# The first four row blocks of v, made by half-height matmuls in two PSUM banks

## The chip, the cores and the metric

The kernel runs on one core of a Trainium2 chip. The metric is the device time of one execution in microseconds (us). The engines are TensorE (PE for its matmuls and PEld for its weight loads, in the profile), VectorE (DVE), ScalarE (ACT), GpSimd (POOL) and SyncE (SP), which issues most of the DMAs. PSUM, into which TensorE writes, has eight banks of 128 partitions x 512 float32.

## The reference

A gate mixes two branches over the same x (2048 rows of 512 columns): a Fourier mixing layer, and sliding-window attention with 32 heads of 16 columns and a window of 256 rows.

```python
def reference(A_x, A_dft_seq_re, A_dft_seq_im, A_dft_hid_re, A_dft_hid_im, B_x, B_wqkv, B_wo, gate_w):
    x = A_x
    g = _sigmoid((x * gate_w).sum(-1, keepdims=True))
    a = _A_ref(x, A_dft_seq_re, A_dft_seq_im, A_dft_hid_re, A_dft_hid_im)   # Real(DFT_seq(DFT_hidden(x)))
    b = _B_ref(x, B_wqkv, B_wo)
    return g * a + (1 - g) * b

def _B_ref(x, wqkv, wo):          # H = 32, Dh = 16, W = 256
    q, k, v = split(x @ wqkv)
    scores = q @ k.T * Dh ** -0.5
    mask = (i - j >= 0) & (i - j < W)
    p = _softmax(where(mask, scores, -1e9))
    return concat_heads(p @ v) @ wo
```

The change touches one product of it alone: v, which is x times the last 512 columns of wqkv, and of its 2048 rows the first 512.

## The kernel before

Every large product is made in float32r, a float32 form that TensorE takes in one pass. To keep precision each operand is split into a rounded part `hi` and a rest `lo`, and three products are summed in PSUM: hi*hi, hi*lo and lo*hi (`TERMS`, L253). x stands in SBUF transposed, in four pieces of 128 contraction rows (`dk`) for each quarter `ss` of the 2048 rows: `XT[dk, ss]` holds hi and lo of such a piece. A block `sb` of v is 128 rows of x (column slice `c` of quarter `ss`) by 512 columns, so it takes 4 pieces x 3 terms = 12 matmuls of 128 contraction rows, a weight block of 128 columns and 512 moving columns, all into one PSUM bank (`row_proj`, L303, the matmul on L309; its tile is called `dv` for v, and `dab` for the Fourier products, which use the same lines). ACT then copies the bank to an SBUF tile `ev` (L320) and SP stores that to the scratch `v_scr` in DRAM (L321).

PSUM is shared out by pools: `ps_a` has four banks (tag `st`, tiles `s` and `t` of the attention), `ps_o` two, `ps_d` two (tag `d`, tiles `dv`, `dqk`, `dab`, `dc`, used in turn).

The program's dense work is one generator, `dense` (L601). It starts with ten matmuls on zeros (`warm`), then the first q and k projection (`qk_first`, 24 matmuls into two banks of `ps_a`), and then, for each quarter of x, the q and k projection (`qk_proj`, from the second quarter on) and four blocks of v. PE, ACT, DVE and SP run in the order in which the code emits the work (`manual_schedule`). The first attention step comes after `need(("v", 5))` (L1003), so up to there PE has dense matmuls only: q and k of the first quarter, v blocks 0 to 3, q and k of the second quarter, v blocks 4 and 5. Later, every few dense matmuls are followed by one of the attention's score matmuls (L372, tile `s`), transposed score matmuls (L454, tile `t`) or a set of its products with v (L480, tile `o`).

While v blocks 0 to 3 run, small jobs are taken from a list (`job`, called after each matmul with its number): one split of a piece of the next quarter's x per block (`x_job`), in which ACT makes `hi` (L80) and DVE makes `lo` (L85). These pieces, `XT[0..3, 1]`, are what the q and k projection right behind the four blocks reads.

The sets of L480 are the only matmuls of the program that use part of TensorE's array: for the four heads `p` of a group, a weight block of 128 rows x 32 columns each, written to the PSUM partitions 32p to 32p+31.

Of the kernel before, what the change touches and what calls it, by code (L numbers as in the profile page):

```python
# [7 lines left out]
F32 = mybir.dt.float32  # L8
# [6 lines left out]
P = 128  # L15
S = 2048
D = 512
DK = D // P
# [14 lines left out]
def fnet_window_mix(ctx: ExitStack, tc: tile.TileContext, xT, x, wqk, wv, wr, wi, cr, ci, wo, gw, out):  # L33
    nc = tc.nc
# [3 lines left out]
    st = ctx.enter_context(tc.tile_pool(name="st", bufs=3))  # L38
    ev = ctx.enter_context(tc.tile_pool(name="ev", bufs=5))
    at = ctx.enter_context(tc.tile_pool(name="at", bufs=2))  # L40
    ps_a = ctx.enter_context(tc.tile_pool(name="ps_a", bufs=4, space=PSUM))
    ps_o = ctx.enter_context(tc.tile_pool(name="ps_o", bufs=2, space=PSUM))
    ps_d = ctx.enter_context(tc.tile_pool(name="ps_d", bufs=2, space=PSUM))
# [4 lines left out]
    v_scr = [dram.tile([2, P, 2, NG, 64], F32, name=f"v_scr{i}") for i in range(8)]  # L48
# [6 lines left out]
    def ld(dst, src):  # L55
        mark("sp", nc.sync.dma_start(dst, src))

    def f(ap):
        return ap.bitcast(F32)
# [4 lines left out]
    def mark(e, ins):  # L64
        last[e] = ins.ins
# [30 lines left out]
    def load_raw(src):  # L96
        raw = st.tile([P, 1024], F32, name="raw", bufs=2)
        ld(raw, src)
        return raw
# [11 lines left out]
    def split_soon(raw, on_dve=False):  # L111
        hi = st.tile([P, 1024], F32R, name="hi")
        lo = st.tile([P, 1024], F32R, name="lo")
        for c in HALVES:
            jobs.append(lambda c=c: late(nc.scalar.copy if FIN else (nc.vector if masks else nc.gpsimd).tensor_copy,
                                         hi[:, c], raw[:, c]))
            jobs.append(lambda c=c: late((nc.vector if on_dve or masks else nc.gpsimd).tensor_sub, lo[:, c], raw[:, c], f(hi[:, c])))
        return hi, lo

    def job(n):  # L120
        if n == 2 and ended:
            ended.pop(0)()
        if n % 6 == 3 and jobs:
            jobs.pop(0)()
# [4 lines left out]
    XT = {}  # L129
# [17 lines left out]
    with tc.manual_schedule(engines={mybir.EngineType.Activation, mybir.EngineType.DVE, mybir.EngineType.SP}):  # L147
# [11 lines left out]
        for dk in range(DK):  # L159
            c = slice(dk * 256, dk * 256 + 256)  # L160
# [92 lines left out]
    TERMS = ((0, 0), (0, 1), (1, 0))  # L253
# [25 lines left out]
    def qk_proj(g, ss, w):  # L279
        for i in range(2):  # L280
            ps = ps_d.tile([P, 512], F32, name="dqk", tag="d")
            n = 0
            for dk in range(DK):
                c = dk * 256 + i * 128
                for a, b in TERMS:
                    nc.tensor.matmul(ps, w[a][:, c:c + 128], XT[dk, ss][:, b],  # L286
                                     start=n == 0, stop=n == 11)
                    n += 1
                    job(n)
                    if n < 12:  # L290
                        yield
            qk_evict(g, ss, i, ps)
            yield
# [9 lines left out]
    def row_proj(sb, w, ps):  # L303
        n = 0
        ss, c = divmod(sb, 4)
        for dk in range(DK):
            wh = [w[dk // 2][h][:, (dk % 2) * 512:(dk % 2) * 512 + 512] for h in range(2)]
            for a, b in TERMS:
                nc.tensor.matmul(ps, XT[dk, ss][:, a, c * 128:(c + 1) * 128], wh[b],  # L309
                                 start=n == 0, stop=n == 11)  # L310
                n += 1
                job(n)
                if n < 12:
                    yield

    def v_proj(sb, w):
        ps = ps_d.tile([P, 512], F32, name="dv", tag="d")
        yield from row_proj(sb, w, ps)
        t = ev.tile([P, 512], F32, name="ev")
        mark("act", nc.scalar.copy(t, ps))  # L320
        ld(v_scr[sb // 2][sb % 2].rearrange("r a g x -> r (a g x)"), t)  # L321
        yield

    def load_ab(i, sc):
        t = big.tile([P, 2, 512], F32R, name="big")
        ld(f(t[:]), ab_scr[i][sc])
        return t
# [263 lines left out]
    def late(fn, *args):  # L591
        with behind("act", "dve"):
            return fn(*args)  # L593
# [7 lines left out]
    def dense():  # L601
# [5 lines left out]
        wvs = [late(split_raw, r, True) for r in wraw]  # L607
# [4 lines left out]
        def x_job(ss, dk):  # L612
            late(split_x, ss, (dk,), ss == 1 or (None if ss == 3 else False))
            if dk % 2 and ss == 2:
                load_x(3, dk // 2)

        for ss in range(4):
            if ss < 3:
                for dk in range(DK):
                    jobs.append(lambda ss=ss, dk=dk: x_job(ss + 1, dk))  # L620
                    jobs.append(lambda: None)
            if ss:
                yield from qk_proj(0, ss, wq0)
            if ss == 3:
                w = split_soon(raw, True)
                jobs[:] = [j for split in jobs for j in (split, lambda: None)]
            for c in range(4):
                yield from v_proj(ss * 4 + c, wvs)
                have.add(("v", ss * 4 + c))
                if c == 1:  # L630
                    have.add(("qk", 0, ss))
                if ss == 2 and c == 2:
                    raw = load_raw(wqk[1])
                    wraw = [load_raw(wi[0])]
# [3 lines left out]
        for g in range(1, NG):  # L638
# [37 lines left out]
            if g < 3:  # L676
                w = nextw
# [20 lines left out]
        for sc in range(4):  # L698
            ab[sc] = load_ab(0, sc)
# [24 lines left out]
        def next_b():  # L724
            if next(calls) * 8 % (2 * SWITCH) >= 8:
                return
            sc = todo_b.pop(0)
            with behind("sp"):
                nxt[sc] = load_ab(1, sc)
# [235 lines left out]


    stream = dense()
    quota = 0.0

# [150 lines left out]
```

## Time and profile before

| | |
|---|---|
| time, median of 3 runs | 844.1 us (843.34 to 844.24) |
| the profiled execution: its own time / its span | 843.79 us / 841.8 us |
| v blocks 0 to 3 on PE | 11.0 to 21.9 us from the span's start |
| PE busy, matmuls and weight loads | 837.9 us in 5322 and 698.4 us in 5322 instructions |
| DVE, ACT, POOL busy | 643.1, 610.1, 294.9 us |

A row of a timeline gives the start, the time from the first start to the last end, the engine, the line of the kernel, the operation with the tile it writes and those it reads, and how many instructions were merged. What stands in square brackets is the idle time of the engine before it, and what ended that. A matmul's own duration contains its way through the array, so matmuls in a row overlap; how fast they follow each other is read from their starts. The chain of waits gives the same work without that overlap.

### The profile page before, as it was taken

Reading aid. Unit: us, or ns where it says so; the run is one execution under the profiler, and the core shown is the slowest. Engines: PE = TensorE matmul, PEld = TensorE weight load, DVE = VectorE, ACT = ScalarE, POOL = GpSimd, SP = SyncE. Lnnn points to the kernel's source line nnn. Section 1 sums busy time; section 2 is a strip of 40 time slices with the busy share of each in tenths; the row PEclk is TensorE's granted clock in tenths of the full one; section 3 lists DMA queues with packets and bytes.
Section 4 is the critical chain, followed back from the end, with each engine's and each line's share of the span. In section 5 each row is a group of like instructions: output and inputs, shape, how many; then the busy total and the mean of one; then the engine's idle time right before and its main releaser. Section 6 shows DMA issues by size and latency. Waiting matters only on the chain.

```text
span 841.8 us, 17198 instructions
## 1 busy us (share of the span) xinstructions
PE 837.9 (100%) x5322; PEld 698.4 (83%) x5322; DVE 643.1 (76%) x2084; ACT 610.1 (72%) x1832; POOL 294.9 (35%) x604
## 2 busy tenths in 40 slices
PE   9999999999999999999999999999999999999998
PEld 8888888888888888888888887878888878878997
DVE  5588977777879787787877876878987867656974
ACT  6488888878888897787877877867877865553330
POOL 8101333233332233342323243343143357756410
PEclk9999999999999999999999999999999999999999
DMA  8776678485756183533454557969864256456632
GB/s 301 249 225 205 209 237 282 158 273 194 231 206 197 46 235 111 175 116 122 140 163 124 167 160 221 299 217 317 277 200 155 96 175 196 143 195 203 206 133 93
DMA packets 94491, 161.03 MB, mean 191 GB/s; under 512 B 26816, under 2 KB 35520, under 8 KB 94400
## 3 DMA queue, kind: packets, MB, share of 16 engines
q1 hardware_dynamic: 93968, 159.28, 58.9%
q8 instruction: 42, 0.69, 0.3%
q10 hardware_dynamic: 432, 0.66, 0.2%
q14 instruction: 49, 0.40, 0.1%
HBM read 108.27 MB, written 51.64 MB: 190 GB/s over the span
## 4 chain that ended last, share of the span: by engine, by line
PE 100%; DVE 0%; issue 0%
PE dc L534 42%; PE dab L309 11%; PE dqk L286 10%; PE t L454 9%; PE s L372 9%; PE o L480 8%; PE dv L309 5%; PE t L929 5%; PE s L274 1%; PE dv L599 1%; PE s L392 0%; PE t L564 0%; DVE rt L566 0%
## 5 line engine op out<-in xcount | busy, mean ns | idle before, releaser
L534 PE MATMUL dc<-big,hi 128*128 128x512 f32 x1020 | 344.3, 393 | 0.0
L374 DVE CUSTOM_DVE_ANT_0 sm<-s,mask 128x320 f32<-128x320 f32 (+4 forms) x512 | 235.1, 464 | 111.0 <-PE s L372 71.1
L377 ACT ACTIVATE sm<-sm,ml 128x320 f32<-128x320 f32 (+4 forms) x512 | 277.3, 543 | 56.2 <-DVE ml L374 52.4
L455 ACT ACTIVATE pt<-t 128x320 f32<-128x320 f32 (+4 forms) x392 | 159.5, 411 | 83.5 <-PE t L454 78.2
L534 PE MATMUL dc<-big,lo 128*128 128x512 f32 x510 | 200.0, 392 | 0.0
L534 PEld LDWEIGHTS dc<-big,hi 128*128 128x128 f32 x1020 | 179.4, 188 | 21.2
L459 POOL TENSOR_SCALAR_AFFINE_SELECT pt<-pt 128x128 f32<-128x128 f32 x196 | 75.7, 386 | 278.2 <-ACT pt L455 276.1
L454 PE MATMUL t<-ring,pad 128*128 128x320 f32 (+4 forms) x512 | 156.6, 306 | 0.0
L372 PE MATMUL s<-ring,pad 128*128 128x320 f32 (+4 forms) x512 | 155.0, 303 | 0.0
L355 DVE TENSOR_SCALAR pad<-ring,half 96x256 fp32r<-96x256 f32 x384 | 118.7, 356 | 5.2 <-PE t L454 4.9
L454 PEld LDWEIGHTS t<-ring,pad 128*128 128x128 f32 x512 | 96.0, 188 | 30.4 <-issue 8.7
L372 PEld LDWEIGHTS s<-ring,pad 128*128 128x128 f32 x512 | 96.2, 188 | 20.3 <-DVE ml L374 0.7
L534 PEld LDWEIGHTS dc<-big,lo 128*128 128x128 f32 x510 | 95.9, 188 | 11.9
L593 DVE TENSOR_TENSOR lo<-raw,hi 128x512 fp32r<-128x512 f32 x139 | 95.9, 697 | 2.5 <-ACT hi L593 2.4
L377 ACT ACTIVATION_READ_ACCUMULATOR sm<-sm,ml 128x1 f32 x512 | 97.3, 190 | 0.0
L309 PE MATMUL dab<-hi,big 128*128 128x512 f32 x256 | 88.9, 394 | 0.0
L286 PE MATMUL dqk<-big,hi 128*128 128x512 f32 x240 | 85.0, 393 | 0.0
L437 POOL TENSOR_SCALAR vpad<-vr,half 128x256 f32<-128x256 f32 x64 | 62.1, 981 | 60.4 <-PE o L480 29.5
L353 ACT ACTIVATE pad<-ring,half 96x256 fp32r<-96x256 f32 x128 | 66.8, 522 | 0.0
L459 POOL TENSOR_SCALAR_AFFINE_SELECT home<-home 128x128 f32<-128x128 f32 x60 | 33.9, 565 | 89.8 <-ACT home L455 85.3
L463 POOL TENSOR_SCALAR_AFFINE_SELECT pt<-pt 128x128 f32<-128x128 f32 x172 | 63.0, 366 | 0.0
L593 DVE CAST hi<-raw 128x512 fp32r<-128x512 f32 x126 | 53.9, 435 | 11.9 <-PE dc L534 10.6
(121 smaller groups left out, 1034.0 us busy)
## 6 DMA issues: line engine op xcount, KB each, us to landing
qk_scr<-home SPq DMA_DIRECT2D x32, 512.0 KB
ring<-qk_scr SPq DMA_DIRECT2D x32, 512.0 KB
raw<-cr SPq DMA_DIRECT2D x32, 512.0 KB
raw<-ci SPq DMA_DIRECT2D x32, 512.0 KB
r_scr<-ev SPq DMA_DIRECT2D x42, 256.0 KB
ab_scr<-home SPq DMA_DIRECT2D x20, 512.0 KB
big<-ab_scr SPq DMA_DIRECT2D x20, 512.0 KB
ring<-qk_scr SPq DMA_DIRECT2D x32, 256.0 KB
```

The source lines that it names most:

```text
L286: nc.tensor.matmul(ps, w[a][:, c:c + 128], XT[dk, ss][:, b], start=n == 0, stop=n == 11)
L309: nc.tensor.matmul(ps, XT[dk, ss][:, a, c * 128:(c + 1) * 128], wh[b], start=n == 0, stop=n == 11)
L355: mark(f"pad{i}", nc.vector.tensor_scalar(dst, src, half[:96, h:h + 1], None, op0=OP.mult))
L372: nc.tensor.matmul(ps[:, :w], PAD[0, n][:, p], ring[1][:, p, k0:k0 + w], start=True, stop=True)
L374: mark("dve", nc.vector.tensor_tensor_reduce(out=sm[:, :w], in0=ps[:, :w], in1=mask[:, WIN - w:], scale=1.0, scalar=3e38, op0=OP.add, op1= ...
L377: mark("act", nc.scalar.activation(sm[:, :w], sm[:, :w], AF.Exp, bias=nm[:, c], scale=-1.0, accum_out=l[:, c]))
L454: nc.tensor.matmul(ps[:, :w], PAD[1, n][:, p], ring[0][:, p, q0:q0 + w], start=True, stop=True)
L455: nc.scalar.activation(pt[:, p, :w], ps[:, :w], AF.Exp, scale=-1.0)
L459: nc.gpsimd.affine_select(a, a, pattern=[[0, 2], [2, 64]], compare_op=OP.is_ge, fill=0.0, base=1, channel_multiplier=-1)
L480: nc.tensor.matmul(OT[g, sb][32 * p:32 * p + 32, q - sb * 512:e - sb * 512], v2[:, p], pt[:, p, q - q0:e - q0], start=first, stop=kb == 8 ...
L534: nc.tensor.matmul(ps, w[a][:, i % 8 * 128:i % 8 * 128 + 128], ab[SC[i]][:, b], start=i == ends[0] and a + b == 0, stop=i == ends[1] and a ...
L593: return fn(*args)
```

## The change

Blocks 0 to 3 of v go through a new function. It takes a second PSUM bank, from `ps_a`, and cuts each of the twelve matmuls in two: contraction rows 0 to 63 into the first bank, rows 64 to 127 into the second. `tile_position` puts the two on the upper and on the lower half of TensorE's array. At the end ACT copies the first bank, as before, and DVE adds the second bank to it. All other blocks of v keep the old function.

```diff
+    def v_first(sb, w):
+        ps = ps_d.tile([P, 512], F32, name="dv", tag="d"), ps_a.tile([P, 512], F32, name="s", tag="st")
+        n = 0
+        ss, c = divmod(sb, 4)
+        for dk in range(DK):
+            for a, b in TERMS:
+                for i in range(2):
+                    r = slice(64 * i, 64 * i + 64)
+                    nc.tensor.matmul(ps[i], XT[dk, ss][r, a, c * 128:(c + 1) * 128],
+                                     w[dk // 2][b][r, (dk % 2) * 512:(dk % 2) * 512 + 512],
+                                     start=n == 0, stop=n == 11, tile_position=(64 * i, 0))
+                n += 1
+                job(n)
+                if n < 12:
+                    yield
+        t = ev.tile([P, 512], F32, name="ev")
+        mark("act", nc.scalar.copy(t, ps[0]))
+        mark("dve", nc.vector.tensor_add(t, t, ps[1]))
+        ld(v_scr[sb // 2][sb % 2].rearrange("r a g x -> r (a g x)"), t)
+        yield
+
...
             for c in range(4):
-                yield from v_proj(ss * 4 + c, wvs)
+                yield from (v_proj if ss else v_first)(ss * 4 + c, wvs)
                 have.add(("v", ss * 4 + c))
```

On PE, the end of the last of the four blocks and the first row of the projection behind it; `dv` is the bank from `ps_d`, `s` the one from `ps_a`, `hi` and `lo` are the weights of v, and `big` the piece of x. Before:

```order
L309 MATMUL dv_440<-hi_332,big_249 128x512
L309 MATMUL dv_440<-hi_332,big_256 128x512
L309 MATMUL dv_440<-lo_333,big_256 128x512
L309 MATMUL dv_440<-hi_332,big_256 128x512
L286 MATMUL dqk_459<-big_378,hi_230 128x512 x2
```

and with the change:

```order
L332 MATMUL dv_482<-hi_332,big_249 128x512
L332 MATMUL s_483<-hi_332,big_249 128x512
L332 MATMUL dv_482<-hi_332,big_256 128x512
L332 MATMUL s_483<-hi_332,big_256 128x512
L332 MATMUL dv_482<-lo_333,big_256 128x512
L332 MATMUL s_483<-lo_333,big_256 128x512
L332 MATMUL dv_482<-hi_332,big_256 128x512
L332 MATMUL s_483<-hi_332,big_256 128x512
L286 MATMUL dqk_515<-big_382,hi_230 128x512 x2
```

Each matmul has become two, which write different banks in turn; over the four blocks that is 96 where there were 48. The rows of PE before and behind the four blocks are the same in both programs.

On DVE, between the first quarter's q and k and the second's, the L85 rows that read `pt` make the `lo` of x's second quarter (tiles `big`), and the L82 and L85 rows that read `raw` split its third quarter. With the change:

```order
L90 TENSOR_TENSOR home_304<-s_339,home_304 128x512 [waits Activation_49]
L85 TENSOR_TENSOR big_382<-pt_322,big_382 128x512 [waits DMAHW1_49,Activation_49]
L341 TENSOR_TENSOR ev_403<-ev_403,s_375 128x512 [waits PE_49,Activation_49]
L85 TENSOR_TENSOR big_415<-pt_322,big_415 128x512 [waits Activation_49]
L341 TENSOR_TENSOR ev_436<-ev_436,s_408 128x512 [waits PE_49,Activation_49]
L85 TENSOR_TENSOR big_457<-pt_324,big_457 128x512 [waits DMAHW2_49,Activation_49]
L341 TENSOR_TENSOR ev_478<-ev_478,s_441 128x512 [waits PE_49,Activation_49]
L85 TENSOR_TENSOR big_490<-pt_324,big_490 128x512 [waits Activation_49]
L341 TENSOR_TENSOR ev_511<-ev_511,s_483 128x512 [waits PE_49,Activation_49]
L82 CAST big_519<-raw_370 128x512 [waits DMAHW3_49]
```

The four L341 rows are new; without them the list is that of before. Each waits for PE and for ACT's copy, and has the next split of x behind it.

On SP, the stores of v, and the loads into `ring` (q and k of the first quarter, from which the attention starts); the rows with a minus are those of before:

```order
 L56 DMA qk_scr_0_0_97<-home 128x2x512 [waits DMAHW6_49,DVE_49]
-L56 DMA v_scr_113<-ev 128x512 [waits Activation_49] x2
+L56 DMA v_scr_113<-ev 128x512 [waits DVE_49] x2
 L56 DMA ring_264<-qk_scr_0_0_81 64x4x512 [waits DMAHW5_49,DMAHW1_49]
-L56 DMA ring_264<-qk_scr_0_0_81 32x4x512 [waits DMAHW2_49]
-L56 DMA ring_265<-qk_scr_0_0_97 32x4x512 [waits DMAHW6_49,DMAHW3_49]
+L56 DMA ring_265<-qk_scr_0_0_97 32x4x512 [waits DMAHW6_49,DMAHW2_49]
+L56 DMA ring_264<-qk_scr_0_0_81 32x4x512 [waits DMAHW3_49]
```

The stores of v wait for DVE where they waited for ACT, and two of the ring's four loads have changed places.

## The prediction

> **What bounds the kernel now.** I read the page's busy times and its chain of waits first, since they say which engine the end hangs on, then the chain in the first 60 us, where the change sits, and then the timelines of PE, DVE and ACT there.
>
> ```profile
> PE 837.9 (100%) x5322; PEld 698.4 (83%) x5322; DVE 643.1 (76%) x2084; ACT 610.1 (72%) x1832; POOL 294.9 (35%) x604
> PEclk9999999999999999999999999999999999999999
> PE 100%; DVE 0%; issue 0%
> 11.18 10.88 PE dv L309 x48
> 22.06 5.44 PE dqk L286 x24
> ```
>
> The first row counts busy time by engine, the second is the clock that TensorE was granted in 40 slices (full speed in all), the third the chain that ended last: all of it is PE. So the time is the sum of what PE's instructions take, one behind the other, and a microsecond more or less on PE anywhere is a microsecond at the end. The last two rows are the chain where the change is: the 48 matmuls of v's blocks 0 to 3 take 10.88 us, which is 226.7 ns each, and the 24 of the next projection 5.44 us, the same 226.7 ns. PE waits for nothing there. Other engines matter only if they come too late for it.
>
> **What a matmul consists of.** PE's timeline in two places gives the parts. The first three rows are from where the attention starts, with a score matmul of 64 columns among those of v; the last two from a later stretch, with 320 columns.
>
> ```profile
> 33.01 0.19 PE L372 MATMUL s<-ring,pad 128*128 128x64 f32 x1
> 33.04 0.47 PE L309 MATMUL dv<-lo,big 128*128 128x512 f32 x1
> 33.35 0.62 PE L309 MATMUL dv<-hi,big 128*128 128x512 f32 x2
> ...
> 120.32 0.31 PE L454 MATMUL t<-ring,pad 128*128 128x320 f32 x1
> 120.47 0.62 PE L309 MATMUL dab<-hi,big 128*128 128x512 f32 x2
> ```
>
> 320 columns hold PE for 0.15 us and 512 for 0.227, so a column costs (0.227 - 0.15) / 192 = 0.40 ns, 512 columns 0.205 us, and about 0.02 us of a matmul is fixed. The 64-column matmul and the one behind it take 33.35 - 33.01 = 0.34 us together, where columns and fixed parts would ask for 0.03 + 0.23 = 0.26: the weights of the second were not there yet. A load of 128 weight columns therefore needs about 0.03 + 0.08 = 0.11 us, and behind a matmul of 512 columns (0.227 us) it is hidden.
>
> **The change on PE.** 48 matmuls go, 96 come. Each has half the contraction rows, but the same 128 weight columns and the same 512 moving columns; nothing above says that rows cost time, and columns do. Alone, each should cost what L309 costs now. The question on which everything hangs is whether the two of a pair run side by side, on the two halves of the array. The trace has one group that does run side by side, the products with v on quarters of the array. Here is one such group with its neighbours, eight sets of four:
>
> ```profile
> 116.85 0.39 PE L309 MATMUL dab<-hi,big 128*128 128x512 f32 x1
> 117.17 2.36 PE L480 MATMUL o<-pt,vpad 128*32 128x320 f32 x32
> 119.46 0.41 PE L454 MATMUL t<-ring,pad 128*128 128x320 f32 x1
> 119.71 0.31 PE L372 MATMUL s<-ring,pad 128*128 128x320 f32 x1
> 119.86 0.39 PE L309 MATMUL dab<-hi,big 128*128 128x512 f32 x1
> ```
>
> 32 matmuls in 2.36 us from first start to last end is 0.27 to 0.29 us for a set of four, although one alone, with its own duration of 0.43 us, would not be through: four overlap. So PE can run tiles side by side. But that group differs from the pair in two ways. Its four write to 32 PSUM partitions each, all different, so that together each partition gets one stream of 320 values in some 0.27 us. The pair of the change writes two banks of the same 128 partitions, so side by side each partition must take 2 x 512 values in 0.227 us, more than three times the rate of that row and twice that of L309; no row of the trace shows this. And the group is plain float32, with 0.27 us for 320 columns against 0.15 us for the float32r of the rest; every float32r matmul in the trace uses the whole array. So the price of a pair is bounded from both sides: as much as one matmul now (side by side), or twice that (one behind the other). By operands, type, columns and the partitions written, the row nearest to a half is L309 itself, and I take twice:
>
> - the pairs: 48 x (2 x 226.7 - 226.7) ns = 48 x 0.2267 = +10.9 us;
> - two changes of the array's layout. From whole to quarters, 117.17 - 116.85 = 0.32 us where 0.227 is usual, 0.09 lost, and with 128 weight columns (that group has 32) up to 0.11 us of load that nothing hides. Back, the last set starts 2.36 - 0.43 = 1.93 us after 117.17, so at 119.10; L454 follows after 0.36 us in place of 0.27, 0.09 lost, and the next matmul comes 0.25 us later where 320 columns take 0.15, 0.10 lost: 0.2 + 0.2 = +0.4 us.
>
> The sum is made against the profiled execution's own 843.79 us (its span is 841.8, and 2.0 lie around it): 843.79 + 10.88 + 0.4 = 855.1 us. The median shown is 844.1, 0.3 above that execution. If the fixed part falls away in a tile, a pair takes 2 x 0.205, +8.8 in place of +10.9: 853.0. If each half adds some 0.01 us, +1.0: 856. So 853 to 856 in this case.
>
> The Trainium skill says otherwise. Its page "TensorE: Matmul & The Clock Gate", section "Part 3: Packing small matmuls — row/col tiling", has matmuls on different row groups of the array run concurrently, and gives 3.07 times the speed for four tiles of 32 rows at 512 columns. By it a pair would cost about what one matmul costs now, and the sum would be 844.2 us; that is the first rival. The trace agrees for tiles that share the columns out (L480, four in 0.27 us), and no run here shows it for tiles that share the rows out, nor for float32r.
>
> **The change on the other engines.** DVE gets four adds of 128 x 512 out of PSUM; the nearest row is L90, 0.68 us each. Their dates are tightest if PE keeps its pace, so I check them there; with slower pairs every block of PE comes 2.7 us later than the one before it and there is more room. DVE, then ACT:
>
> ```profile
> 12.18 0.68 DVE L92 SCALAR_TENSOR_TENSOR home<-s,home 128x512 fp32r<-128x512 f32 x1
> 12.78 0.68 DVE L90 TENSOR_TENSOR home<-s,home 128x512 fp32r<-128x512 f32 x1
> 13.38 0.68 DVE L85 TENSOR_TENSOR big<-pt,big 128x512 fp32r<-128x512 f32 x1
> 15.08 0.69 DVE L85 TENSOR_TENSOR big<-pt,big 128x512 fp32r<-128x512 f32 x1 [1.02 <-ACT big L80]
> 20.19 0.70 DVE L85 TENSOR_TENSOR big<-pt,big 128x512 fp32r<-128x512 f32 x1 [4.42 <-ACT big L80]
> 21.19 0.69 DVE L85 TENSOR_TENSOR big<-pt,big 128x512 fp32r<-128x512 f32 x1 [0.31 <-ACT big L80]
> 21.80 0.42 DVE L82 CAST big<-raw 128x512 fp32r<-128x512 f32 x1
> 25.45 0.69 DVE L92 SCALAR_TENSOR_TENSOR home<-dqk,home 128x512 fp32r<-128x512 f32 x1 [2.50 <-ACT home L88]
> ```
>
> ```profile
> 16.66 0.59 ACT L320 COPY ev<-dv 128x512 f32<-128x512 f32 x1 [1.61 <-PE dv L309]
> 20.06 0.58 ACT L320 COPY ev<-dv 128x512 f32<-128x512 f32 x1
> 22.10 0.59 ACT L320 COPY ev<-dv 128x512 f32<-128x512 f32 x1 [0.94 <-PE dv L309]
> ```
>
> The adds fall into the idle 1.02, 4.42 and 2.50 us. The third one, after ACT's copy at 20.64 and DVE's L85 at 20.89, ends at 21.57 and moves the last L85 from 21.19 to 21.57, so the last `lo` of x's second quarter is there at 22.3. PE reads that in the tenth to twelfth matmul of the projection that starts at 22.06, so not before 22.06 + 10 x 0.227 = 24.3: 2 us to spare. If that cover were gone, the price would be 0.4 us, once. The fourth add (copy done at 22.69, so 23.4) has L82 and L85 behind it, which are through by 24.5, before L92 at 25.45. The new PSUM banks are those of the first projection; DVE has read them out by 13.5, and the third block, first to take one again, starts after 16.
>
> SP's stores of v wait 0.7 us longer, and the loads of `ring` stand behind two of them.
>
> ```profile
> L56 SPq DMA_DIRECT2D ring<-qk_scr x4: 566/617/787, 19.3 to 21.2; - x4
> 30.91 0.60 DVE L355 TENSOR_SCALAR pad<-ring,half 96x256 fp32r<-96x256 f32 x2
> 33.24 0.23 DVE L374 CUSTOM_DVE_ANT_0 sm<-s,mask 128x64 f32<-128x64 f32 x1 [1.73 <-PE s L372]
> ```
>
> The loads are issued at 19.3 to 21.2; the second store's data would be there at 17.25 + 0.68 = 17.9, still before. Whoever reads the ring (L355, at 30.91) did not wait for it, and after that DVE waits 1.73 us for PE. So these edits cost nothing.
>
> **The rivals.** *Side by side* (not slower): the second of a pair starts while the first streams, on its own half of the array and into its own bank. Place: the four blocks; price: a pair as long as one matmul, 48 x 0 + 0.4 = 844.2 us, with 843.2 if a pair needs only the 0.205 us of its columns (48 x -0.022 = -1.0) and 845.2 if it pays the fixed 0.02 us twice. It decides if a pair takes under 226.7 + 1.7 / 48 = 262 ns; then the time is within 0.2%. For it: L480 shows tiles side by side, two weight loads of 0.11 us fit behind 0.227, and the two banks differ. Against it: the rate per PSUM partition, and the type. *Half hidden* (slower): the pair overlaps, but one weight load of it, 0.11 us, finds no cover: 48 x 0.11 = 5.3, with the 0.4 849.5 us; other partial overlaps lie at 846 to 853. For it: a load is hidden now by its neighbour's columns alone. Against it: in L480 loads are hidden among tiles, since a set takes no longer than its columns' 0.27 us. *Faster by over 0.2%*: 1.7 us from 48 pairs would need pairs of under 0.19 us, less than 512 columns take in any row; only an effect on the rest of the program that I don't see could do it.
>
> **How the numbers follow.** One behind the other 0.45 (853 to 856), half hidden 0.12, side by side 0.38, faster 0.03, and 0.02 for more than 856. The predicted time is that of the likeliest, 855.1. The cases lie apart, so the range has to span them, from 843.2, the low end of side by side, to 856.0. 0.2% of the time, 1.7 us, is about what a measurement of this kernel can tell from no change. Slower by more than that: 0.45 + 0.12 + 0.02 = 0.59; within it 0.38; faster 0.03.
>
> **What would show it.** In PE's timeline from 11 us: starts of the two halves some 0.22 us apart, and the four blocks over 22 us long, ending near 33, would bear me out; starts a few ns apart with pairs every 0.23 us, and the projection L286 beginning at 22.3, would be side by side; pairs every 0.33 us, half hidden. The rest of the chain should keep its lengths. Idle time of PE ahead of L286 or of the first L372, with DVE or a DMA as releaser, would prove the part on the other engines wrong. The prediction as a whole fails if the pairs overlap.

## The result, and the profile after

The kernel with the change takes 845.6 us (median of 18 runs, 844.01 to 846.88), the kernel before beside it 844.04 us (18 runs, 843.26 to 844.7): 1.002 times as long, with a 95% interval of 1.0012 to 1.0027. The profiled execution took 845.55 us with a span of 843.6, against 843.79 and 841.8 before. So the change loses some 1.6 us, and not the 11.3 of the forecast.

The first rows of the page of the changed kernel: busy time by engine, the chain that ended last, and the group of the q and k projection with the idle time before it.

```profile
PE 838.8 (99%) x5370; PEld 698.0 (83%) x5370; DVE 647.7 (77%) x2088; ACT 609.7 (72%) x1832; POOL 295.5 (35%) x604
...
PE 98%; DVE 1%; DMA 1%; issue 0%; SPq 0%
...
L286 PE MATMUL dqk<-big,hi 128*128 128x512 f32 x240 | 85.3, 394 | 0.9 <-DVE home L90 0.6 <-DVE home L92 0.3
```

PE has 48 matmuls more and is busy only 0.9 us longer. The chain, all PE before, now has a per cent of DVE and one of DMA, and L286 waits 0.9 us for DVE. Before, it waited for nothing:

```profile
L286 PE MATMUL dqk<-big,hi 128*128 128x512 f32 x240 | 85.0, 393 | 0.0
```

Two things are to be explained: 48 matmuls that cost almost nothing, and a wait in work that the change does not touch.

**The pairs.** PE's timeline of the changed kernel, where the four blocks begin and end:

```profile
10.29 0.61 PE L274 MATMUL s<-big,hi 128*128 128x512 f32 x2
10.84 0.49 PE L332 MATMUL dv<-hi,big 64*128 64x512 f32 x1
10.84 0.49 PE L332 MATMUL s<-hi,big 64*128 64x512 f32 x1
11.17 0.39 PE L332 MATMUL dv<-lo,big 64*128 64x512 f32 x1
11.18 0.39 PE L332 MATMUL s<-lo,big 64*128 64x512 f32 x1
...
21.42 0.39 PE L332 MATMUL dv<-lo,big 64*128 64x512 f32 x1
21.42 0.39 PE L332 MATMUL s<-lo,big 64*128 64x512 f32 x1
21.65 0.39 PE L332 MATMUL dv<-hi,big 64*128 64x512 f32 x1
21.65 0.39 PE L332 MATMUL s<-hi,big 64*128 64x512 f32 x1
21.96 0.73 PE L286 MATMUL dqk<-big,hi 128*128 128x512 f32 x2
22.53 0.40 PE L286 MATMUL dqk<-big,lo 128*128 128x512 f32 x1
```

The two of a pair start together, and the next pair 0.23 us later: a pair holds PE as long as one whole matmul did. Only the ends show, in the same way at both. The first pair starts 0.32 us behind the last whole matmul ahead of it (10.52, the second of the row at 10.29) where 0.227 is usual, the second pair 0.33 us behind the first, and some ten more pairs lose another 0.05 together: 0.25 us. L286 starts 0.32 us behind the last pair, its second matmul 0.33 us later, the next ten lose 0.05: 0.25 us again. Against the last matmul ahead of v, PE is 0.49 us later by 28 us than in the kernel before, and the same 0.49 stands in all eight profiles here of kernels that make the four blocks in pairs, 0.00 in those of whole matmuls.

**The rest.** Set each start of PE beside the start of the same matmul in the kernel before, and the difference is PE's slip. It is 0.22 us from 28 to 85 us (the matmul ahead of v began 0.28 earlier, and the 0.49 are on top), 0.91 at 95 us, 1.53 at 105 us and 1.74 at the end. So 1.3 us come within 20 us, far behind the change. The first place, in the timelines of the kernel before (GpSimd's split of the weights `wi`, and DVE's pads with the eviction L92 behind them):

```profile
83.86 0.61 DVE L355 TENSOR_SCALAR pad<-ring,half 96x256 fp32r<-96x256 f32 x2
84.38 0.68 DVE L92 SCALAR_TENSOR_TENSOR home<-dqk,home 128x512 fp32r<-128x512 f32 x1
84.60 0.61 POOL L593 CAST hi<-raw 128x512 fp32r<-128x512 f32 x1 [3.85 <-DVE pad L355]
85.17 2.55 POOL L593 TENSOR_TENSOR lo<-raw,hi 128x512 fp32r<-128x512 f32 x2
```

and of the changed one, with PE:

```profile
84.01 0.61 POOL L614 CAST hi<-raw 128x512 fp32r<-128x512 f32 x1 [3.04 <-DMA raw<-wi]
84.07 2.00 DVE L376 TENSOR_SCALAR pad<-ring,half 96x256 fp32r<-96x256 f32 x2
84.58 2.63 POOL L614 TENSOR_TENSOR lo<-raw,hi 128x512 fp32r<-128x512 f32 x2
85.99 0.68 DVE L92 SCALAR_TENSOR_TENSOR home<-dqk,home 128x512 fp32r<-128x512 f32 x1
86.05 0.39 PE L286 MATMUL dqk<-big,lo 128*128 128x512 f32 x1
86.72 0.51 PE L286 MATMUL dqk<-big,hi 128*128 128x512 f32 x1 [0.28 <-DVE home L92]
```

The order has turned round. Before, the split starts 0.74 us behind the first pad, when the pads are through; with the change, 0.06 us ahead of it, and the two pads take 2.00 us in place of 0.61 (0.69 and 1.38, where one usually takes 0.34). L92, which empties the bank that PE wants next, comes 1.4 us later against PE's work, and PE stands still. Ten microseconds on it happens again, with the spreading of v over `vpad` on GpSimd. Before, then with the change:

```profile
93.03 1.83 POOL L437 TENSOR_SCALAR vpad<-vr,half 128x256 f32<-128x256 f32 x2 [2.36 <-DMA vr<-v_scr]
94.70 0.87 DVE L355 TENSOR_SCALAR pad<-ring,half 96x256 fp32r<-96x256 f32 x3
```

```profile
95.16 1.85 POOL L458 TENSOR_SCALAR vpad<-vr,half 128x256 f32<-128x256 f32 x2 [2.89 <-DMA vr<-v_scr]
95.77 1.39 DVE L376 TENSOR_SCALAR pad<-ring,half 96x256 fp32r<-96x256 f32 x3
97.08 0.67 DVE L90 TENSOR_TENSOR home<-dqk,home 128x512 fp32r<-128x512 f32 x1
```

Before, GpSimd was nearly through (94.86) when the three pads began; now it works beside them, they take 1.39 us in place of 0.87, and PE waits for L90. Two rows of PE's waits in the changed kernel, with the us in total, the times and the longest; before there was neither:

```profile
PE dqk L286 <- DVE home L90: 0.6, 1, 0.6
PE dqk L286 <- DVE home L92: 0.3, 1, 0.3
```

**Why the order turned.** What GpSimd waits for at both places is a load. Among the DMAs of the changed kernel there is a queue of their own for PE's instructions:

```profile
q8 instruction: 42, 0.69, 0.4%
```

42 packets of 16 KB for 5370 matmuls and 5370 weight loads, so some 256 instructions each. They come when PE has used up so many, and 96 instructions more move them: at 20.8, 49.2, 75.7 and 101.3 us before, at 18.4, 36.8, 63.4 and 91.2 us with the change. Before, the load of `wi`, issued at 78.47 us, had 15 of its 16 parts by 83.42 and the last at 84.45; with the change, issued at 78.70, it had 15 by 83.63 and was whole at 83.86. GpSimd began 0.15 us behind the last part both times. The load of `vr`, the other way round, took 2.3 us from issue to GpSimd's start before and 2.9 with a fetch at 91.2 just ahead of it. A theory, then: the pairs are free, the change of layout costs 0.49 us, and 1.3 us come from two collisions of DVE's pads with GpSimd, into which the extra PE instructions shift the loads.

### The profile page after: what moved, and what is told of

Its sections match the earlier page's. It is cut to its first block, busy times and chain, and to the rows that moved or that the text cites. A ratio compares the mean times of both kernels' runs of the same rounds, so it can differ in the third digit from the quotient of the medians.

```text
span 843.6 us, 17302 instructions
## 1 busy us (share of the span) xinstructions
PE 838.8 (99%) x5370; PEld 698.0 (83%) x5370; DVE 647.7 (77%) x2088; ACT 609.7 (72%) x1832; POOL 295.5 (35%) x604
## 4 chain that ended last, share of the span: by engine, by line
PE 98%; DVE 1%; DMA 1%; issue 0%; SPq 0%
PE dc L555 42%; PE dab L309 11%; PE t L475 9%; PE dqk L286 9%; PE s L393 8%; PE o L501 8%; PE t L950 5%; PE dv L309 4%; PE dv L332 1%; PE s L274 1%; PE dv L620 1%; DMA raw<-wqk 1%; PE s L413 0%; PE t L585 0%; DVE pad L376 0%
## 5 line engine op out<-in xcount | busy, mean ns | idle before, releaser
L480 POOL TENSOR_SCALAR_AFFINE_SELECT pt<-pt 128x128 f32<-128x128 f32 x196 | 77.2, 394 | 274.2 <-ACT pt L476 270.9
L376 DVE TENSOR_SCALAR pad<-ring,half 96x256 fp32r<-96x256 f32 x384 | 121.0, 361 | 5.2 <-PE t L475 5.0
L309 PE MATMUL dab<-hi,big 128*128 128x512 f32 x256 | 88.9, 394 | 0.0
L286 PE MATMUL dqk<-big,hi 128*128 128x512 f32 x240 | 85.3, 394 | 0.9 <-DVE home L90 0.6
L480 POOL TENSOR_SCALAR_AFFINE_SELECT home<-home 128x128 f32<-128x128 f32 x60 | 32.8, 548 | 91.0 <-ACT home L476 86.0
```

Of the source, the lines that this page charges most:

```text
L286: nc.tensor.matmul(ps, w[a][:, c:c + 128], XT[dk, ss][:, b], start=n == 0, stop=n == 11)
L376: mark(f"pad{i}", nc.vector.tensor_scalar(dst, src, half[:96, h:h + 1], None, op0=OP.mult))
L480: nc.gpsimd.affine_select(a, a, pattern=[[0, 2], [2, 64]], compare_op=OP.is_ge, fill=0.0, base=1, channel_multiplier=-1)
```

## The experiments

A slip is PE's start against the same matmul of the profiled kernel before. Each ratio is to runs of the kernel before beside it.

**The adds without the pairs.** Twelve whole matmuls per block, six into each bank; banks, adds and stores as in the change.

```diff
-                for i in range(2):
-                    r = slice(64 * i, 64 * i + 64)
-                    nc.tensor.matmul(ps[i], XT[dk, ss][r, a, c * 128:(c + 1) * 128], ...
+                nc.tensor.matmul(ps[dk // 2], XT[dk, ss][:, a, c * 128:(c + 1) * 128],
+                                 w[dk // 2][b][:, (dk % 2) * 512:(dk % 2) * 512 + 512],
+                                 start=n % 6 == 0, stop=n % 6 == 5)
```

> The four blocks with whole 128-row matmuls again, the contraction's first half into the one bank and its second half into the other; DVE's four adds, the stores that wait for DVE and the order of the ring's loads are those of the change. PE has as many instructions as before and changes its layout nowhere. Theory 1 (two changes of the array's layout cost 0.4 us; the other 1.2 us come from 96 more PE instructions, which move the points at which PE's next 16 KB of instructions are fetched by DMA, so that a weight load lands earlier, GpSimd starts on it just before DVE's pads instead of behind them, and PE waits for DVE at 86 and 96 us): 844.0 us within 0.3, fetches at 20.8, 49.2 and 75.7 us as before, no idle PE ahead of L286. Theory 2 (the adds and the later stores cost the 1.2 us): 845.2 us.

843.92 us, 0.9998 times before (0.9989 to 1.0007). v took 11.107 us as before, the split of `wi` started behind the pads. The second bank, the adds and the stores cost nothing.

**96 PE instructions in the kernel before.** Matmuls on zeros in the warm-up, which also start v later.

```diff
-WARM = 10
+WARM = 4
+EXTRA = 30
...
+        for i in range(EXTRA):
+            nc.tensor.matmul(ps[:32, :16], zero[:, :32], zero[:, :16], start=True, stop=True)
```

> The kernel before with 96 more PE instructions in the warm-up, which runs while the first data is on its way: 4 instead of 10 large matmuls on zeros, and 30 tiny ones (16 columns). v is made as before. Theory 1: the fetches move by 96 instructions, as in the change (18.4, 36.8, 63.4, 91.2 us), GpSimd's split at 84 us comes before DVE's pads, PE idles some 1 us ahead of L286 at 86 and 96 us: 845.2 us, apart from what the shorter warm-up does to the first projection, which its start shows. Theory 2: 844.0 us, since nothing of DVE's and SP's work has changed.

847.64 us, 1.0039 (1.0025 to 1.0053); v starts 2.80 us later, which leaves 844.84. The fetches came at 65.7 and 93.5 us, and the collisions of the changed kernel appeared in a kernel that has no pairs; its timeline at the first place, and its row of PE's waits, which is of the second:

```profile
86.65 1.65 DVE L356 TENSOR_SCALAR pad<-ring,half 96x256 fp32r<-96x256 f32 x2
86.78 2.67 POOL L594 TENSOR_TENSOR lo<-raw,hi 128x512 fp32r<-128x512 f32 x2
```

```profile
PE dqk L287 <- DVE home L91: 0.5, 1, 0.5
```

The slip grew by 0.92 us from 85 to 105 us.

**160 more in the kernel with the change,** 256 in all, so that the fetches fall near their old place.

```diff
-WARM = 10
+WARM = 0
+EXTRA = 50
```

> The change with 160 more PE instructions in the warm-up (no large matmul on zeros, 50 tiny ones), so that with its own 96 there are 256 more than before, as many as one fetch of 16 KB holds. Theory 1: the fetches come at the points of the kernel before again, only one more at the start, and the wait at 86 and 96 us goes: 844.4 us, plus what a colder start costs the first projection. Theory 2: 845.6 us plus the same.

847.06 us, 1.0032 (1.002 to 1.0045); the matmul ahead of v starts 2.25 us later, which leaves 844.8. Fetches at 52.0, 78.5 and 103.5 us; the pads go ahead of GpSimd again:

```profile
86.60 0.61 DVE L377 TENSOR_SCALAR pad<-ring,half 96x256 fp32r<-96x256 f32 x2
87.04 0.64 POOL L615 CAST hi<-raw 128x512 fp32r<-128x512 f32 x1 [3.54 <-DVE pad L377]
```

PE waited for DVE nowhere; the slip grew by 0.16 from 85 us to the end. With the run before, the loss follows the number of PE instructions and not the pairs.

**No adds.** The output lacks half the contraction in the first 512 rows of v.

```diff
-        mark("dve", nc.vector.tensor_add(t, t, ps[1]))
```

> The change without DVE's four adds: the second bank is filled but not added, so that the first 512 rows of v lack half of their contraction. PE's instructions are those of the change. Theory 1: 845.6 us, the same wait ahead of L286. Theory 2: 844.4 us, the two changes of layout alone.

845.84 us, 1.0021 (1.0012 to 1.003): the loss stays without the adds. The collision was there (second pad 1.38 us), with 0.59 us of slip from 85 to 105 us; another 1.0 us came at 735 us, where PE waited for ACT, which stays unexplained.

**The second split of wi off GpSimd.** Emitted behind the next pads, where DVE makes it near 100 us; in the changed kernel, then in the one before.

```diff
-                        ws.append(split_soon(wraw[1]))
+                        ws.append(split_soon(wraw[1], pad=True))
...
                 make_pad(0, n + 1)
+                with behind("pad0"):
+                    while pad_jobs:
+                        pad_jobs.pop(0)()
```

> The change, with the four operations that split the second half of wi taken from their place in the list of jobs and emitted behind the next pad of DVE; there the attention has begun its second part, so all four go to DVE, and GpSimd has only the rest of the first half to split, which no longer stands behind a load. GpSimd and DVE's pads should no longer meet at 84 us. Theory 1: no idle PE ahead of L286 at 86 us, and what is left of the loss are the two changes of layout: 844.4 us, 0.4 above the same edit of the kernel before. A rival, that PE's loss at 86 us has another cause (the larger PE program, the later stores of v): 845.6 us, 1.6 above the same edit of the kernel before.

> The same edit in the kernel before, as the one to compare with. Theory 1: 844.0 us within 0.3, since there GpSimd came behind the pads anyway; DVE's 1.1 us more work at 98 us could cost a little. The rival: the same.

845.16 us with the change, 1.0012 (1.0004 to 1.0021), and 844.36 before, 0.9998 (0.9989 to 1.0007): 0.8 apart where 0.4 was expected. The wait for L92 was gone; the one for L90 stayed, 0.2 us, beside `vpad`:

```profile
94.09 1.83 POOL L467 TENSOR_SCALAR vpad<-vr,half 128x256 f32<-128x256 f32 x2 [2.97 <-DMA vr<-v_scr]
95.06 1.26 DVE L385 TENSOR_SCALAR pad<-ring,half 96x256 fp32r<-96x256 f32 x3
```

So the second collision is not a mere consequence of the first. Of its slip of 0.46 us from 95 to 105 us, the edit itself makes 0.16, as the same edit in the kernel before shows.

**More changes of layout.** Pairs for two of the four pieces only, the other two whole: eight ways into pairs and back in place of one.

```diff
-                for i in range(2):
-                    r = slice(64 * i, 64 * i + 64)
+                for i in range(2 - dk % 2):
+                    r = slice(64 * i, 64 * i + 64) if dk % 2 == 0 else slice(0, 128)
...
-                                     start=n == 0, stop=n == 11, tile_position=(64 * i, 0))
+                                     start=n == 0, stop=n == (11, 8)[i], tile_position=(64 * i, 0))
```

> The change with its pairs in the pieces dk 0 and 2 alone; dk 1 and 3 are whole matmuls into the first bank again. TensorE changes its layout 16 times in the four blocks in place of 2. If a way in and back costs 0.4 us, as the change's own trace has it (0.20 in, 0.19 back), the stretch from the first matmul of v to the second of the next projection is 8 x 0.4 = 3.2 us longer than in the kernel before, 2.8 longer than in the change. If the cost is one of starting and ending the four blocks and not of the layout, it stays at 0.4. PE has 48 more instructions than before, so that the fetches lie between those of the two kernels; the wait at 86 us may come or not.

849.2 us, 1.0054 (1.004 to 1.0067). From the first matmul of v to the second of L286 it took 14.463 us, where it was 11.106 before; with what is lost ahead of and behind that, PE is 3.46 us later: 0.43 us for each way there and back.

**Quarters.** Blocks 0 and 2 in four tiles of 32 rows and four banks, blocks 1 and 3 whole.

```diff
-                for i in range(2):
-                    r = slice(64 * i, 64 * i + 64)
+                for i in range(4):
+                    r = slice(32 * i, 32 * i + 32)
...
-                yield from (v_proj if ss else v_first)(ss * 4 + c, wvs)
+                yield from (v_proj if ss or c % 2 else v_first)(ss * 4 + c, wvs)
```

> Blocks 0 and 2 in four tiles of 32 rows, each into a bank of its own (two of them from the attention's output banks, not yet in use), added by three adds of DVE; blocks 1 and 3 whole. It tests the step that failed: if a PSUM partition takes values for several banks at once without limit, the four of a set start within some 15 ns and a set takes 0.227 us, as a pair does. If two streams are the most (the bound that I had set at one), a set takes 0.45 us and each of the two blocks 5.4 us in place of 2.7. If four weight loads of 0.11 us have to follow one another, 0.43 us a set.

846.1 us, 1.0021 (1.0012 to 1.003). PE's timeline:

```profile
12.17 0.39 PE L333 MATMUL dv<-hi,big 32*128 32x512 f32 x1
12.18 0.38 PE L333 MATMUL s<-hi,big 32*128 32x512 f32 x1
12.18 0.39 PE L333 MATMUL o<-hi,big 32*128 32x512 f32 x2
12.40 0.39 PE L333 MATMUL s<-lo,big 32*128 32x512 f32 x1
...
14.02 0.38 PE L333 MATMUL dv<-hi,big 32*128 32x512 f32 x1
14.33 0.50 PE L309 MATMUL dv<-hi,big 128*128 128x512 f32 x1
```

Four start within some 10 ns, and the next four 0.228 us later. (In the other block in quarters one of the four starts 0.11 us behind the rest, but the sets follow each other as fast.) Neither four streams into the same PSUM partitions nor four weight loads take longer than one.

**240 more PE instructions out of the matmuls themselves.** Quarters in blocks 0 to 2, halves in block 3, so that the fetches return to their place without a longer warm-up.

```diff
+        cut = 2 if sb == 3 else 4
...
-                for i in range(2):
-                    r = slice(64 * i, 64 * i + 64)
+                for i in range(cut):
+                    r = slice(h * i, h * i + h)
```

> Blocks 0 to 2 in four tiles of 32 rows and block 3 in two of 64, ten adds on DVE; the warm-up is left as it is. It has 240 more PE instructions than the kernel before, nearly the 256 of one fetch, against 96 in the change. More of what the change does (tiles, banks, adds, stores that wait for DVE), so a theory that the loss lies in these asks for at least the change's 845.6 us. Theory 1: the fetches come back to where they were in the kernel before (some 2 us later), GpSimd's split at 84 us comes behind DVE's pads again, PE does not idle ahead of L286, and what is left is the way in and back and one change from 32-row to 64-row tiles, 0.4 + 0.2: 844.6 us, between 844.3 and 845.0.

845.77 us, 1.0022 (1.0013 to 1.0032): missed. The part at issue went as expected: fetch at 78.4 us, the split behind the pads, no slip from 85 to 105 us. But v took 12.255 us, since the third block had to wait for a bank (its second set starts 0.44 us behind its first, once DVE is done with the first block) and the tiles changed once more, and 0.5 us were lost near 115 us, for a cause that the trace does not settle.

**The change once more.** No edit.

> The change itself once more, beside the run above on the same chip: 845.6 us; in its trace GpSimd's split before DVE's pads at 84 us and idle PE ahead of L286, as in the first profile, if Theory 1's order of the two is settled by the program and not by chance.

845.53 us, 1.0018 (1.0009 to 1.0026): fetches at 63.8 and 92.6 us, the split 0.22 us ahead of the pads, slip 1.14 from 85 to 105 us. The collision belongs to the program.

**The load alone.** No PE instruction more: the load of `wi` is cut into four DMAs, with the half that GpSimd needs first ahead (early) or last (late).

```diff
+            for i in order:
+                ld(raw[:, i * 256:i * 256 + 256], src[:, i * 256:i * 256 + 256])
...
-                        wraw.append(load_raw(wi[1]))
+                        wraw.append(load_raw(wi[1], (0, 1, 2, 3)))
```

For late the order is (2, 3, 0, 1).

> The kernel before; only the load raw<-wi, issued at 78.5 us, is cut into four DMAs of 256 columns, in the order 0, 1, 2, 3, so that the first half, for which GpSimd's first cast waits, lands earlier. No instruction of PE is added, its instruction fetches keep their dates. Theory 1 (the order of GpSimd's split and DVE's pads near 84 us makes the loss): GpSimd starts ahead of or among the pads, a pad takes about 1.4 us, PE waits for L92 or L90 as in the kernel with the change, slip of PE over 85 to 105 us +0.5 to +1.2, time 844.5 to 845.2. Theory 2 (the loss comes from the fetches or from something else that the added PE instructions do): no loss, 843.9 to 844.2.

> The same with the four DMAs in the order 2, 3, 0, 1: the first half lands last, some tenths of a us later than in one DMA. Both theories: GpSimd starts behind the pads as before, 843.9 to 844.3; it shows what the cutting alone costs.

> The change with the same cut, in the order 0, 1, 2, 3: GpSimd's split starts ahead of the pads as it does already. Both theories: the loss stays, 845.2 to 845.8.

> The change with the order 2, 3, 0, 1: the half that GpSimd waits for lands later, some 84.5 us or after. Theory 1: the split starts behind the pads, no wait at 86 us; if the collision there is all, 844.3 to 844.5; if it is half, as the run with the split moved to DVE suggests, 844.8 to 845.1. Theory 2: the loss stays, 845.4 to 845.7.

Kernel before, early: 844.11 us, 1.0005 (0.9996 to 1.0014); late: 844.36, 1.0006 (0.9997 to 1.0014). With the change, early: 846.9, 1.0038 (1.0025 to 1.005); late: 846.2, 1.0033 (1.0021 to 1.0046). Two of the four did not do what they were made for. The early one before only got the split to 83.80 us, still 0.18 behind the first pad: the second pad met its CAST alone and took 0.70 us, and PE lost nothing. With the change, the late one let the split begin at 83.82, no later than in one DMA. But the early one with the change tells much, by a miss of its own:

```profile
83.77 0.61 POOL L618 CAST hi<-raw 128x512 fp32r<-128x512 f32 x1 [2.58 <-PE s L397]
84.29 2.79 DVE L380 TENSOR_SCALAR pad<-ring,half 96x256 fp32r<-96x256 f32 x2
84.34 2.59 POOL L618 TENSOR_TENSOR lo<-raw,hi 128x512 fp32r<-128x512 f32 x2
86.27 0.39 PE L290 MATMUL dqk<-big,lo 128*128 128x512 f32 x1
...
87.00 0.68 DVE L92 SCALAR_TENSOR_TENSOR home<-dqk,home 128x512 fp32r<-128x512 f32 x1
87.73 0.50 PE L290 MATMUL dqk<-big,hi 128*128 128x512 f32 x1 [1.07 <-DVE home L92]
```

The split got 0.52 us ahead of the pads in place of 0.06, so that both pads met a TENSOR_TENSOR and took 2.79 us. The slip from 85 to 95 us was 1.47 in place of 0.69, with the fetches near where they had been (63.4 and 92.4 us). It is the order of the two engines that makes the loss, whatever sets the order. (This profiled execution also waited for ACT near 735 us, another 1.0 us, as the one without the adds did.)

**Both collisions taken away.** The split as above, and the second `vpad` pair made by DVE, after the projection (it ran at 123 us); in the changed kernel and in the one before.

```diff
-            nc.gpsimd.tensor_scalar(v2[:, :, :, 16 * h:16 * h + 16], ...
+            (nc.vector if n == 4 else nc.gpsimd).tensor_scalar(v2[:, :, :, 16 * h:16 * h + 16], ...
...
+            if k == 4 and p == 2:
+                with behind("dve", "act", "pad1"):
+                    v_spread(4)
+                v_next(8)
```

> The change with both of GpSimd's pieces of work taken from beside DVE's pads: the split of wi as in the run with the split moved to DVE, and besides the second vpad pair (L458, 95.16 us in the changed kernel) is made by DVE, behind a later L92, near 110 us. No instruction of PE is added or moved. Theory 1 (the two collisions of pads with GpSimd make the 1.2 us, one at 84 to 86 us, one at 95 to 97 us): no pad over 0.4 us between 84 and 99 us, PE waits neither for L92 nor for L90, slip over 85 to 105 us 0 to 0.1; time 844.4 to 844.7, or as much over it as the same edit costs in the kernel before. Theory 2 (something else that the added PE instructions bring): the slip over 95 to 105 us stays at 0.4 to 0.6, 845.0 to 845.5.

> The same edit in the kernel before, where neither piece collides: it shows what the edit itself costs. Both theories: 843.9 to 844.5; two more instructions on DVE near 110 us may add up to 0.5 us if the L92 behind them comes too late for PE.

845.02 us with the change, 1.0007 (0.9998 to 1.0016), and 844.53 before, 1.0002 (0.9993 to 1.001), beside 844.49 for the kernel before. The timeline of the changed one:

```profile
84.74 0.61 DVE L385 TENSOR_SCALAR pad<-ring,half 96x256 fp32r<-96x256 f32 x2
85.26 0.68 DVE L92 SCALAR_TENSOR_TENSOR home<-dqk,home 128x512 fp32r<-128x512 f32 x1
...
95.45 0.87 DVE L385 TENSOR_SCALAR pad<-ring,half 96x256 fp32r<-96x256 f32 x3
96.23 0.68 DVE L90 TENSOR_TENSOR home<-dqk,home 128x512 fp32r<-128x512 f32 x1
```

The pads have the lengths of before, PE waits for DVE nowhere, and the slip grows by 0.10 us from 85 to 105 us, though the fetches stand at 63.8 and 92.1 us as in the change. The profiled execution slipped another 1.36 us later on, without a wait that repeats. That leaves 0.49 us between the two medians, which 11 runs each give to some tenths, and the layout asks for 0.49.

All runs side by side, from their traces: how far behind (+) or ahead (-) of the first pad of its pair the split began, the longest pad at the first place (83 to 92 us) and at the second (from 94 us), and what the slip grew at each:

| kernel | split | longest pad, 1st | slip 85 to 95 us | longest pad, 2nd | slip 95 to 105 us |
|---|---|---|---|---|---|
| before | +0.74 | 0.71 | - | 0.35 | - |
| whole matmuls | +0.82 | 0.79 | 0.00 | 0.35 | 0.06 |
| before, load early | +0.18 | 0.70 | 0.00 | 0.48 | 0.09 |
| before, load late | +0.71 | 0.68 | 0.17 | 0.34 | 0.08 |
| change, 160 more | +0.44 | 0.44 | 0.00 | 0.48 | 0.16 |
| change, 240 more | +0.56 | 0.52 | 0.00 | 0.35 | -0.03 |
| before, split off | none | 0.35 | 0.00 | 0.35 | 0.16 |
| before, both off | none | 0.35 | 0.00 | 0.35 | 0.21 |
| change, both off | none | 0.35 | 0.00 | 0.35 | 0.09 |
| change, split off | none | 0.35 | 0.00 | 0.55 | 0.46 |
| quarters | -0.32 | 1.38 | 0.45 | 0.35 | -0.10 |
| change | -0.06 | 1.38 | 0.69 | 0.55 | 0.62 |
| change again | -0.22 | 1.38 | 0.60 | 0.56 | 0.54 |
| change, load late | -0.08 | 1.37 | 0.68 | 0.55 | 0.54 |
| change, load early | -0.52 | 1.50 | 1.47 | 0.56 | 0.49 |
| change, no adds | -0.44 | 1.38 | 0.26 | 0.53 | 0.33 |
| before, 96 more | -0.44 | 1.39 | 0.35 | 0.55 | 0.57 |
| more changes of layout | -0.29 | 1.38 | 0.54 | 0.57 | 0.50 |

Wherever the split began ahead of the pads, a pad took 1.37 us or more and PE lost 0.26 us or more; wherever it began behind the first of them or was gone, no pad took over 0.79, and PE lost nothing but 0.17 in one run. A long pad is not the loss by itself: in the four runs with the split taken off, a pad of 1.38 us stands near 81 us, beside the split of the first half of `wi`, and PE's slip did not change there. At the second place pads of 0.53 us or more go with 0.33 us or more lost, shorter ones with at most 0.21; the two places come apart in two rows ("split off" and "quarters").

## Why the prediction was wrong

**The failed step is the price of a pair.** I wrote: "By operands, type, columns and the partitions written, the row nearest to a half is L309 itself, and I take twice". 48 pairs at 453 ns were to cost +10.9 us. The pairs follow each other after 0.228 us on average (0.224 to 0.236 behind the second), so that the term is nothing that the ends do not hold already. Both reasons for it fell: the quarters wrote four streams of 512 values into the same 128 PSUM partitions in 0.228 us, so the rate per partition was no limit at twice, nor at four times; and float32r matmuls run in tiles as the float32 of L480 do. A limit that no row showed had been given more weight than the one row that showed tiles at work. The rule that I had set against it, that of the Trainium skill's "TensorE: Matmul & The Clock Gate" in "Part 3: Packing small matmuls — row/col tiling", has row groups run concurrently, and the trace agrees, for two tiles and for four.

**The changes of layout** were put at 0.4 us; they took 0.49 in the change, and 0.43 each way there and back where there were eight. The forecast had the two late starts at each end nearly to the number (0.09 and 0.11); what it left out is the 0.05 that the ten matmuls behind them lose. Whether the 0.11 is a weight load, as it assumed, no run tells.

**DVE's adds, the second bank and SP's stores** were put at nothing, which the whole matmuls in two banks bear out (843.92 us), and the loss that stayed without the adds.

**The rival "side by side"** had the mechanism, with 844.2 us, 843.2 to 845.2. It fell short by 1.4 us: 0.09 of layout and 1.3 that it had at nothing. That missing term stood in my own text as a sentence: "The rest of the chain should keep its lengths." I had followed the added work as far as 33 us, on DVE, ACT and SP, and nothing of it was late there. What I had not priced is that 96 PE instructions are fetched by DMA too, and that the margin between two engines at 84 us was 0.74 us. Sum by the profiled execution: -0.28 at the start and +0.49 layout, which make 0.22 unrounded, +0.69 and +0.62 at the two collisions, +0.21 behind 105 us: 1.74, which is the slip at the end.

**What is shown and what is inferred.** That the collisions make the 1.3 us is shown: with both pieces off GpSimd's path they are gone, and with the load early the first one doubles. That the number of PE instructions decides on them is shown by adding 96 without pairs and 160 with them. That it does so through the fetches, by delaying a load, is inferred, but from more than one trace. In 14 of the profiles `wi` is one DMA. In the six with a fetch at 75.4 to 78.5 us (before, whole matmuls, 160 more, 240 more, and the kernel before with one or both off) it took 5.67 to 6.05 us from issue to landing, and the last of its 16 parts came 0.55 to 1.03 us behind the fifteenth. In the eight without (96 more in the kernel before among them) it took 4.78 to 5.16, and the last part was 0.23 behind at most. By these numbers, without that late part the split would begin ahead of the pads there too. But no run moved a fetch by itself, and the trace does not name the DMA engine that a packet went through. "Half hidden" (849.5 us) is out, since the pairs follow each other as fast as whole matmuls.

**Readings ahead of the result that are off,** without moving the forecast. L480 is not the only line on part of the array: the 32 matmuls of L392 (`s<-ident,mlh`, 128*64) are float32r with 64 weight columns, though one behind the other. A plain float32 matmul leaves two records in the trace (L480: the program makes 704, the trace has 1408), so the 32 at 117 us are 16 matmuls; that four records start together holds. And the 64-column matmul has its fixed 0.02 us too, so 0.28 and not 0.26 was to be expected of it and its neighbour; the 0.11 us for a load stays.

## What to carry to other kernels

Cutting the contraction into row tiles gains nothing where the columns set the pace, but it is free save for some 0.5 us at each way into tiles and back, so keep tiled matmuls together. A change that is neutral on the bounding engine can still lose later: list the places where a second engine has less than a microsecond of margin (here DVE's pads against GpSimd's splits), and ask whether the change moves any load that sets the order there, instruction fetches included. When such a loss appears far from the edit, compare starts of the same instruction in both traces and look where the difference steps.

## What the hardware showed unexpectedly

- Row tiles of float32r run at full overlap: two halves start 4 ns apart, four quarters mostly within 20 ns, and the sets follow each other after 0.228 us, as whole matmuls of 512 columns do after 0.227. A way into tiles and back costs 0.49 us, the same 0.25 at each end.
- A pad on DVE, 0.34 us by itself, ended 0.15 us behind a TENSOR_TENSOR of GpSimd (1.29 to 1.37 us) beside which it had begun, wherever in the first 1.09 us that was: begun 0.11 us into it, the pad took 1.38 us (84.69 us with the change), 0.74 us into it, 0.71 (87.16 before). The Trainium skill's page "SBUF — State Buffer", section "SBUF: two separate sides", has DVE and GpSimd share a pair of ports which the one that starts first gets for its whole instruction, the other blocked, where DVE's instruction runs in a two-port mode or has two inputs in SBUF. The trace agrees in the holding; in which mode the pads ran, no run here shows. Beside GpSimd's `vpad` (0.92 to 1.07 us each) the pads were stretched to 0.57 us at most, not held for its length.
- PE's instructions arrive in packets of 16 KB, 256 at a time, each taking 0.9 to 1.7 us with the change. 96 instructions more moved the later ones 10 to 12 us ahead. Where one had come up to 3 us ahead of the issue of the load of `wi`, the last of its 16 parts came 0.55 to 1.03 us behind the fifteenth.
